# The setup of a fused RWKV and mixture-of-experts kernel in another order, and half of d v on GpSimd in units 1 to 3

## The chip, the cores and the metric

The kernel runs on one core of one Trainium2 chip. The metric is the device time of one execution in microseconds (us); smaller is better. The core has five engines that run beside each other, each through its own list of instructions in order: TensorE (PE; PEld is its weight load), VectorE (DVE), ScalarE (ACT), GpSimd (POOL) and SyncE (SP), which here issues the loads. An instruction waits on semaphores that other engines or finished loads raise, and everything behind it on its engine waits too.

## The reference

Two stages. The first is a linear-attention recurrence for 4 batches, 8 heads, 768 tokens and 48 columns a head. The second sends each of the 3072 token rows (384 wide) to one of 8 experts.

```python
for t in range(S):
    cur = u * k_t (outer) v_t
    y[t] = r_t @ (state + cur)
    state = w * state + k_t (outer) v_t
...
logits = x @ w_gate + modality_bias[modality_id]
e = argmax(logits)
out = prob[e] * (relu(x @ w1[e]) @ w2[e])
```

## The kernel before

The recurrence is computed in chunks of 128 tokens: 4 batches by 6 chunks are 24 units, taken in order 0 to 23 (all batches of chunk 0 first). For a unit, `rc` is r times decreasing powers of w (`powr`) and `kc` is k times increasing ones (`powk`), both with the head's columns on the partitions, two heads to a pair, four pairs (`NPR`) to a tile of 112 partitions by 4 x 128. `scores` multiplies `kc` by `rc` on TensorE into two PSUM banks, `causal` (VectorE) multiplies each by the mask into `at`, `values` (TensorE) multiplies `at` by v into `py`, then the keys `kt` by v into the state's bank `pst`, then `bonus`: the products of `rk` = k r with u, which give the eight numbers `d` of each token. `taken` copies `d` (ScalarE), `own` scales v by it head by head on ScalarE into `dv`, and `token` adds `dv` to `py` (VectorE) and squares it (ScalarE); `factor`, `high` and `low` make the scaled f16 halves of the row. In units of `SHARED` GpSimd makes the second half of `dv` in one product (`shared`) and ScalarE only the first.

From the first unit on, the engines' orders are written by hand (a manual schedule): what stands first in the program is first on its engine. One turn i of the loop over units issues, among others: `keys_turned(i+2)` (transposes of the key rows on TensorE), `scores(i+1)`, `taken(i)`, `shared(i)`, `token(i-1)`, `decay(i+3)` (`rc`, GpSimd), `carry(i+2)` (`kt`, GpSimd), `keys(i+2)` (VectorE), `own_turned(i+2)` (`rk`, VectorE, up to unit 3), `factor(i-1)`, `own(i)`, `high(i-1)`, `causal(i+1)`, `low(i-1)`, `values(i)`.

`setup` comes before the loop. In its program order it does, on each engine:

- SyncE: loads w, unit 0's turned rows (`turned(0)`, r and k, 384 KB into `ud0`), `turned(1)`, u in single elements (`uT`, 384 of them), then the k and v lines of units 0 to 2, `turned(2)`, the gate's weights, bias and modality; at its end unit 3's rows, `turned(4)`.
- VectorE: memsets (`ud0`'s unused rows among them), a running product of w (a scan), the reciprocal, the second half of `powk`, `w128`, then for unit 0 `kc` in two halves, the upper half of `rc`, `rk`, later `causal(0)`, `keys(1)`, `own_turned(1)`.
- ScalarE: its table load, the blank of `ud2`'s unused rows, three copies of powers into `powk` and `powr`, four `wk` scalings, blanks of `ud3`, of the four `kt` and of the state `st[1]`, the copy of `wtok`, `taken(0)`.
- GpSimd: the blank of `ud1`, identity and mask, `counts` (constants for the routing), the lower half of unit 0's `rc` in two quarters, `decay(1)`, the copies of u into `ub`, `carry(0)`, `decay(2)`, `uw`, `carry(1)`.
- TensorE: ten products on ones (`WARM`) that write nothing used, `scores(0)`, four transposes for `wtok`, `keys_turned(1)`, `bonus(0)`; in the loop's first turn `keys_turned(2)`, then three more products on ones (`DENSE`) ahead of `scores(1)`.

After the attention units the experts' weights are split and the rows of each expert are multiplied, mostly bound by TensorE; the change touches nothing there.

Of the kernel before, what the change touches and what calls it, by code (L numbers as in the profile page):

```python
# [37 lines left out]
NQ = 6  # L38
WARM = 10
NJ = 40  # L40
LATE = 5
SHARES = (0, 4), (4, 2), (6, 2)

DENSE = 6
FADED = range(4, 14)
SHARED = range(9, 14)
TURNED = (*range(1, 8), *range(12, 15))
RAISED = range(6, 12)
OWNED = range(17, 24)
GROUPED = 6  # L50
# [13 lines left out]
LOW, TOP = 64 - D, 64 + D  # L64
HALVES = slice(0, 64), slice(64, TOP)


class _Kernel:
# [16 lines left out]
    def setup(self):  # L85

        nc, c = self.nc, self.c
        w = c.tile([P, NPR], F32, name="w")
        nc.vector.memset(w, 1.0)
        nc.sync.dma_start(w[LOW:TOP, :], self.wT.rearrange("j d a -> (j d) a"))  # L90
        uT = c.tile([P, NPR], F32, name="uT")
        self.ud = [c.tile([P, 2 * NPR * P], F32, name=f"ud{q}") for q in range(4)]
# [3 lines left out]
        zero = c.tile([P, P // 2], F32, name="zero")  # L96
        nc.vector.memset(zero, 0.0)
        warm = self.warm = c.tile([P, 512], F16, name="warm")
        nc.gpsimd.memset(warm, 1.0)
        self.ones16 = warm[:, :P]  # L100
        for t in self.kv:
            nc.vector.memset(t[:, :LOW], 0.0)
        nc.vector.memset(self.ud[0][:LOW], 0.0)
        nc.gpsimd.memset(self.ud[1][:LOW], 0.0)
        H2 = P // 2
        blank = lambda t: nc.scalar.copy(t.rearrange("p (a z) -> p a z", z=P // 2), zero[: t.shape[0]].unsqueeze(1).to_broadcast([t.shape[0], t.shape[1] // (P // 2), P // 2]))
        self.tables = c.tile([P, 3, NPR, H2 + 1], F32, name="tables")
        wb, one0, pw = (self.tables[:, q] for q in range(3))
# [4 lines left out]
        nc.vector.memset(one0[:, :, 0:1], 1.0)  # L113
        nc.vector.memset(uT, 0.0)
        blank(self.ud[2][:LOW])
        self.turned(0)
        self.turned(1)
        nc.sync.dma_start(uT[LOW:TOP, :], self.u.rearrange("o (a z) -> z (o a)", a=NPR))
        self.lines(1, 0)
# [3 lines left out]
        for i in range(3):  # L123
            self.lines(i, 1)
        wg = c.tile([P, DC * E], F32, name="wgf")
        nc.sync.dma_start(wg, self.wg)
        bias = c.tile([P, 2 * E], F32, name="bias")
        nc.sync.dma_start(bias, self.bias.to_broadcast([P, 2 * E]))
        mod = c.tile([P, 2 * NT // P], I32, name="mod")
        nc.sync.dma_start(mod, self.mod)  # L130
        self.raw_in = wg, bias, mod

# [6 lines left out]
        self.ones = c.tile([P, P], F32, name="ones")  # L139
        nc.vector.memset(self.ones, 1.0)  # L140
        id32 = self.id32 = c.tile([P, P], F32, name="id32")
        make_identity(nc, id32)
        self.mask = c.tile([P, P], F32, name="mask")
        nc.gpsimd.affine_select(self.mask, self.ones, pattern=[[1, P]], compare_op=ALU.is_gt, fill=0.0, base=0, channel_multiplier=-1)
        self.counts()
        flat = lambda t: t.rearrange("p a z -> p (a z)")
# [14 lines left out]
        p64 = pw[:, :, H2 : H2 + 1].rearrange("p a o -> p (a o)")  # L161
        nc.vector.tensor_mul(self.w128, p64, p64)
        self.ub, self.uw = (c.tile([P, NPR, 2], F32, name=n) for n in ("ub", "uw"))
        self.decay(0, NPR, NPR // 2)
        self.keys(0, 2)
        u = self.ctx_[0]
        nc.vector.tensor_mul(u["rc"][:TOP, NPR // 2 :], u["rT"][:TOP, NPR // 2 :], self.powr[:TOP, NPR // 2 :])
        self.own_turned(0)
        self.decay(1)
        self.scores(0)  # L170
        self.wtok = c.tile([P, NPR, 2 * D], F32, name="wtok")
        wk = []
# [79 lines left out]
    def counts(self):  # L252

        c, v = self.c, self.nc.gpsimd
        self.onesb = c.tile([P, P], BF16, name="onesb")
        v.memset(self.onesb, 1.0)
        self.id16 = c.tile([P, P], F16, name="id16")
        make_identity(self.nc, self.id16)
        self.tok = c.tile([P, NT // P], I32, name="tok")
# [7 lines left out]
        self.base = c.tile([P, E], F32, name="base")  # L267
        v.tensor_copy(self.base, self.cbase)
        self.line = c.tile([P, 1], F32, name="line")
        v.tensor_copy(self.line, self.tok[:, 0:1])  # L270

# [56 lines left out]

    def turned(self, i):
# [5 lines left out]
        self.nc.sync.dma_start(ud[LOW:TOP, :m], self.pd[b * NCH + c].rearrange("j d n -> (j d) n")[:, :m])  # L335
        self.ctx_.setdefault(i, {}).update( rT=ud[:, :n].rearrange("p (a t) -> p a t", a=NPR), kT=ud[:, n:].rearrange("p (a t) -> p a t", a=NPR))
# [55 lines left out]

    def own_turned(self, i):
# [46 lines left out]
    def scores(self, i):  # L440
        nc, u = self.nc, self.ctx_[i]
        u["ps"] = [self.ps_a.tile([P, 512], F32, tag="big", name=f"psc{i}_{j}") for j in range(2)]
        if i == 1:

            for q in range(DENSE // 2):
                nc.tensor.matmul(u["ps"][q % 2], self.ones16, self.warm, start=True, stop=True)

        for pr in range(NPR):
            for q in range(2):
                s = slice(64 * q, 64 * q + 64)  # L450
                for j, r in enumerate(HALVES):
                    nc.tensor.matmul(u["ps"][j][s, pr * P : (pr + 1) * P], u["kc"][r, pr, s], u["rc"][r, pr, :], start=True, stop=True)  # L452
# [712 lines left out]
    def run(self):  # L1165
        nc, tc, m = self.nc, self.tc, self.m
# [233 lines left out]
        i, j = NU - 2, NU - 1  # L1400
# [208 lines left out]
```

## Time and profile before

| what | before |
|---|---|
| median of 3 runs | 334.5 us (333.94 to 335.64) |
| the profiled execution | 336.65 us |
| its span, first to last instruction | 334.6 us |
| busy: PE, PEld | 320.0 us (96%), 263.5 us (79%) |
| busy: DVE, ACT, POOL | 213.5 us (64%), 181.7 us (54%), 159.7 us (48%) |
| mean granted clock of TensorE | 0.994 |
| DMA | 48.71 MB, mean 146 GB/s |

The span is counted from the first instruction; the execution's time has about 2 us more around it. A busy share is an average over the whole span: the setup and the first units are some 30 us of it. Matmul ends are modelled, so a busy PE is not PE at its peak.

### The profile page before, as it was taken

The numbers are of one execution on the slowest core, as the hardware profiler recorded it, in microseconds if no ns is written. First come the engines' busy times: TensorE is split into PE (matmuls) and PEld (weight loads), VectorE is DVE, ScalarE is ACT, GpSimd is POOL, SyncE is SP. The second block draws the span as 40 slices with busy tenths as digits, with TensorE's granted clock in tenths as the row PEclk, the third lists the DMA queues.
The fourth block names the chain that finished last, engine by engine and source line by source line (L and its number), as shares of the span: only waits on it lengthen the run. The fifth ranks groups of instructions, "written<-read, shape, count | busy, mean of one in ns | idle before, by whom it ended". The sixth has DMA issues, their size and how long they took to land. (4 is left out here: it accounts for less than half of the span.)

```text
span 334.6 us, 15202 instructions
## 1 busy us (share of the span) xinstructions
PE 320.0 (96%) x5434; PEld 263.5 (79%) x5434; DVE 213.5 (64%) x727; ACT 181.7 (54%) x500; POOL 159.7 (48%) x241
## 2 busy tenths in 40 slices
PE   7999998998999999999999999999999999999992
PEld 2888897898978888797878788886888877777771
DVE  6878985899988988896667422286333332234950
ACT  7898888789655578676422222274222225543820
POOL 8978863967599886554458212203111111111211
PEclk9999999899999999999999999999999999999999
DMA  6879986995579999954246431119512211122110
GB/s 185 244 171 207 204 250 222 293 229 155 126 197 270 267 223 299 275 156 119 78 106 231 156 78 47 47 47 332 121 50 65 50 47 24 47 56 62 37 47 5
DMA packets 58013, 48.71 MB, mean 146 GB/s; under 512 B 42344, under 2 KB 50807, under 8 KB 57712
## 3 DMA queue, kind: packets, MB, share of 16 engines
q1 hardware_dynamic: 54768, 38.63, 47.5%
q0 software_dynamic: 3200, 9.47, 8.2%
q8 instruction: 30, 0.49, 0.7%
q14 instruction: 15, 0.12, 0.1%
HBM read 27.99 MB, written 11.83 MB: 119 GB/s over the span
## 5 line engine op out<-in xcount | busy, mean ns | idle before, releaser
L1067 PEld LDWEIGHTS <-whi 128*128 128x128 f16 x1248 | 72.6, 98 | 3.6 <-issue 0.7
L1076 DVE SCALAR_TENSOR_TENSOR hl<-phb,hh 128x256 f16<-128x256 f32 (+1 forms) x48 | 24.4, 508 | 66.8 <-ACTq L1540 66.8
L1130 PEld LDWEIGHTS <-hh 128*128 128x128 f16 x416 | 39.1, 98 | 25.3 <-ACT hh L1071 1.2
L1067 PE MATMUL phb<-mxT,whi 128*128 128x128 f16 x768 | 50.7, 219 | 0.0
L438 ACT ACTIVATE dv<-kv,d 128x48 f32<-128x48 f32 x172 | 43.0, 325 | 0.0
L1071 ACT ACTIVATE hh<-phb 128x256 f16<-128x256 f32 (+1 forms) x48 | 21.5, 455 | 32.4 <-PE phb L1067 22.9
L1067 PEld LDWEIGHTS <-wlo 128*128 128x128 f16 x624 | 37.8, 98 | 0.0
L1036 POOL TENSOR_TENSOR seenb<-otb,putb 128x1 int32<-128x1 int32 x16 | 4.1, 257 | 63.0 <-ACTq L1540 50.8
L458 DVE TENSOR_TENSOR at<-psc,mask 128x512 f32<-128x512 f32 x48 | 32.5, 681 | 1.5 <-PE psc L452 1.4
L1130 PEld LDWEIGHTS <-hl 128*128 128x128 f16 x208 | 19.8, 98 | 15.7 <-issue 2.5
L366 POOL TENSOR_TENSOR rc<-ud,powr 112x512 f32<-112x512 f32 (+1 forms) x25 | 30.8, 1237 | 0.2
L1027 ACT ACTIVATE otb<-po,fac 128x384 f32<-128x384 f32 x16 | 9.3, 580 | 39.5 <-PE phb L1067 39.5
L452 PE MATMUL psc<-rc,kc 64*64 64x128 f32 (+1 forms) x768 | 28.5, 281 | 1.2 <-POOL rc L366 1.0
L701 POOL DMA_INDIRECT rows<-row,posi x24 | 24.6, 1026 | 10.2 <-issue 3.6
L1067 PE MATMUL phb<-mxT,wlo 128*128 128x128 f16 x384 | 29.3, 219 | 0.0
L1130 PE MATMUL po<-whi,hl 128*128 128x384 f16 x136 | 28.0, 326 | 1.2 <-PEq L1605 0.7
L1130 PE MATMUL po<-whi,hh 128*128 128x384 f16 x136 | 27.7, 326 | 0.6 <-ACT hh L1071 0.4
L489 PE MATMUL py<-kv,at 128*64 128x48 f32 x768 | 27.0, 222 | 1.2 <-issue 1.2
L1067 PE MATMUL phs<-mxT,whi 128*128 128x128 f16 x432 | 27.3, 219 | 0.6 <-issue 0.6
L1130 PE MATMUL po<-wlo,hh 128*128 128x384 f16 x136 | 27.7, 326 | 0.0
L452 PEld LDWEIGHTS psc<-rc,kc 64*64 64x64 f32 (+1 forms) x768 | 21.9, 135 | 6.5 <-issue 2.5
L489 PEld LDWEIGHTS py<-kv,at 128*64 128x64 f32 x768 | 25.3, 138 | 2.1 <-issue 1.8
(292 smaller groups left out, 625.6 us busy)
## 6 DMA issues: line engine op xcount, KB each, us to landing
kv<-in_pt SPq DMA_DIRECT2D x21, 384.0 KB, 4.8
ud<-in_pd SPq DMA_DIRECT2D x14, 384.0 KB, 5.4
raw<-in_w SPq DMA_DIRECT2D x12, 256.0 KB, 5.1
raw<-in_w SPq DMA_DIRECT2D x6, 512.0 KB, 5.2
raw<-in_w SPq DMA_DIRECT2D x2, 1536.0 KB, 6.5
rows<-pad SPq DMA_DIRECT2D x10, 193.0 KB, 3.6
ud<-in_pd SPq DMA_DIRECT2D x10, 192.0 KB, 3.8
rt<-in_pt SPq DMA_DIRECT2D x7, 192.0 KB, 5.2
```

Source lines behind the costliest of these rows:

```text
L366: nc.gpsimd.tensor_mul(u["rc"][:TOP, s], u["rT"][:TOP, s], self.powr[:TOP, s])
L438: nc.scalar.activation(u["dv"][:, sl], u["v"][:, sl], AF.Copy, scale=u["d"][:, h : h + 1])
L452: nc.tensor.matmul(u["ps"][j][s, pr * P : (pr + 1) * P], u["kc"][r, pr, s], u["rc"][r, pr, :], start=True, stop=True)
L458: nc.vector.tensor_mul(u["at"][:, j * NPR : (j + 1) * NPR, :], u["ps"][j].rearrange("p (q t) -> p q t", q=NPR), self.mask.unsqueeze(1).to_ ...
L489: nc.tensor.matmul(py[t, sl], u["at"][:, j * NPR + pr, t], u["v"][:, sl], start=c == h == 0, stop=h == H - 1, skip_group_check=True)
L701: i = nc.gpsimd.indirect_dma_start(out=self.rows, out_offset=bass.IndirectOffsetOnAxis(ap=u["posi"][:, b : b + 1], axis=0), in_=u["row"][: ...
L1027: self.nc.scalar.activation(ot, po[:, :DM], AF.Copy, scale=gf[:, t : t + 1])
L1036: i1 = nc.gpsimd.tensor_tensor(seen, ot[:, 0:1].bitcast(I32), idx, ALU.add)
L1067: self.nc.tensor.matmul(ph[:, q * P : (q + 1) * P], w[:, c0 : c0 + P], self.xT[:, xq, t * P : (t + 1) * P], start=i == q == 0, stop=i == l ...
L1071: self.nc.scalar.activation(self.hh[:, f0 : f0 + fb, t * P : (t + 1) * P], p3, AF.Relu)
L1076: self.nc.vector.scalar_tensor_tensor(self.hl[:, f0 : f0 + fb, r], p3, 0.0, self.hh[:, f0 : f0 + fb, r], ALU.max, ALU.subtract)
L1130: self.nc.tensor.matmul(po[:, :DM], h[:, f, t * P : (t + 1) * P], w[:, c0 : c0 + DM], start=first, stop=last)
```

## The change

Order and placement change; every result stays. `turned(0)` is issued by ScalarE's queue as its first instruction. u is loaded as 4 rows of 96 (`ux`), transposed by TensorE into PSUM (`psd`) and copied to `ub` by ScalarE. `first` writes unit 0's rows and keys in other pieces: GpSimd one quarter of `rc`, VectorE half of `kc`, half of `rc`, `w128`, half of `kc`, a quarter of `rc`; `scores(0)` takes the pairs in the order 0, 1, 3, 2. Unit 0's `rk` moves from VectorE to GpSimd, behind `decay(1)`. Blanks: `ud0` to ScalarE (from VectorE), `ud2` to GpSimd (from ScalarE), `ud3` and `st[1]` behind `taken(0)`, `kt` ahead of the powers. `counts` is cut in three: `numbers` stays, `masks` comes behind `rk`, the rest at the end. `keys_turned(2)` moves from the loop into the setup, ahead of `bonus(0)`. The three `DENSE` products and one of `WARM` go. The gate's weights, bias and modality are loaded behind unit 3's. `SHARED` gains units 1 to 3.

```diff
-WARM = 10
+WARM = 9
-DENSE = 6
-SHARED = range(9, 14)
+SHARED = (*range(1, 4), *range(9, 14))
...
-        uT = c.tile([P, NPR], F32, name="uT")
...
+        self.turned(0, nc.scalar)
+        self.turned(1)
+        ux = c.tile([NPR, TOP], F32, name="ux")
+        self.ub, self.uw = (c.tile([P, NPR, 2], F32, name=n) for n in ("ub", "uw"))
+        nc.gpsimd.memset(ux, 0.0)
+        nc.gpsimd.memset(self.ub, 0.0)
+        nc.sync.dma_start(ux[:, LOW:], self.u.rearrange("o (a z) -> (o a) z", a=NPR))
-        nc.vector.memset(self.ud[0][:LOW], 0.0)
...
-        nc.vector.memset(uT, 0.0)
-        blank(self.ud[2][:LOW])
-        self.turned(0)
-        self.turned(1)
-        nc.sync.dma_start(uT[LOW:TOP, :], self.u.rearrange("o (a z) -> z (o a)", a=NPR))
+        blank(self.ud[0][:LOW])
+        for t in self.kt:
+            nc.scalar.copy(t[:, :, :LOW], zero[:, : NPR * LOW].rearrange("p (a z) -> p a z", a=NPR))
...
-        nc.vector.memset(self.ones, 1.0)
+        nc.gpsimd.memset(self.ones, 1.0)
...
-        self.counts()
+        nc.gpsimd.memset(self.ud[2][:LOW], 0.0)
+        self.numbers()
...
-        nc.vector.tensor_mul(self.w128, p64, p64)
-        self.ub, self.uw = (c.tile([P, NPR, 2], F32, name=n) for n in ("ub", "uw"))
-        self.decay(0, NPR, NPR // 2)
-        self.keys(0, 2)
-        u = self.ctx_[0]
-        nc.vector.tensor_mul(u["rc"][:TOP, NPR // 2 :], u["rT"][:TOP, NPR // 2 :], self.powr[:TOP, NPR // 2 :])
-        self.own_turned(0)
+        self.first(p64)
         self.decay(1)
+        self.own_turned(0, nc.gpsimd)
         self.scores(0)
...
-        blank(self.ud[3][:LOW])
-        for t in self.kt:
-            nc.scalar.copy(t[:, :, :LOW], zero[:, : NPR * LOW].rearrange("p (a z) -> p a z", a=NPR))
+        self.masks()
+        psd = self.ps_s.tile([P, 512], F32, tag="s", name="psd")
+        nc.tensor.transpose(psd[:TOP, :NPR], ux, id32[:NPR, :NPR])
+        for j, r in enumerate(HALVES):
+            nc.scalar.copy(self.ub[r, :, j], psd[r, :NPR])
+        self.keys_turned(1)
         pt = self.ps_y.tile([P, 512], F32, tag="y", name="pwk")
...
+        self.causal(0, 0)
+        self.keys(1)
+        self.causal(0, 1)
+        self.own_turned(1)
+        self.keys_turned(2)
+        self.bonus(0, psd)
+        self.taken(0)
+        blank(self.ud[3][:LOW])
         blank(self.st[1].rearrange("p b a e -> p (b a e)"))
-        nc.gpsimd.memset(self.ub, 0.0)
-        for j, r in enumerate(HALVES):
-            nc.gpsimd.tensor_copy(self.ub[r, :, j], uT[r])
-        self.keys_turned(1)
-        self.causal(0, 0)
-        self.causal(0, 1)
-        self.keys(1)
-        self.own_turned(1)
         self.carry(0)
         self.decay(2)
...
-        self.bonus(0, pst)
-        self.taken(0)
         self.carry(1)
+        self.counts()
         self.feed(3)
+        wg = c.tile([P, DC * E], F32, name="wgf")
+        nc.sync.dma_start(wg, self.wg)
         self.turned(4)
...
+    def first(self, p64):
+
+        nc, u, half = self.nc, self.ctx_[0], NPR // 2
...
+        part = lambda eng, out, x, pw, s: eng.tensor_mul(u[out][:TOP, s], u[x][:TOP, s], pw[:TOP, s])
+        lo, hi = slice(0, half), slice(half, NPR)
+        part(nc.gpsimd, "rc", "rT", self.powr, slice(NPR - 1, NPR))
+        part(nc.vector, "kc", "kT", self.powk, lo)
+        part(nc.vector, "rc", "rT", self.powr, lo)
+        nc.vector.tensor_mul(self.w128, p64, p64)
+        part(nc.vector, "kc", "kT", self.powk, hi)
+        part(nc.vector, "rc", "rT", self.powr, slice(half, NPR - 1))
...
-        self.nc.vector.tensor_mul(u["rk"][:TOP], u["kT"][:TOP], u["rT"][:TOP])
...
+        (by or self.nc.vector).tensor_mul(u["rk"][:TOP], u["kT"][:TOP], u["rT"][:TOP])
...
-        if i == 1:
-
-            for q in range(DENSE // 2):
-                nc.tensor.matmul(u["ps"][q % 2], self.ones16, self.warm, start=True, stop=True)
-
-        for pr in range(NPR):
+        for pr in range(NPR) if i else (0, 1, 3, 2):
...
-            if i < GROUPED:
+            if 0 < i < GROUPED:
                 each(i + 2, self.keys_turned)
```

## Rows read from the trace of the kernel before

**Rows 1.** Windows: stretch, its us, busy us of PE, PEld, DVE, ACT, POOL, clock, DMA.

```profile
30.00:40.00 10.00, 9.67 (x287) 9.00 (x282) 9.29 (x36) 7.81 (x32) 7.99 (x10) 1.00 1.01 205
```

**Rows 2.** Timeline of the setup, TensorE: start, us, engine, line, operation, idle before.

```profile
8.07 0.42 PEld L182 LDWEIGHTS pwk<-id,wk 128*128 128x128 f32 x4 [0.17 <-ACT kt L179]
9.09 0.55 PEld L413 LDWEIGHTS psd<-ub,rk 112*64 112x64 f32 x16 [0.18 <-POOL ub L187]
10.04 0.42 PEld L446 LDWEIGHTS <-warm 128*128 128x128 f16 x3
10.88 1.10 PE L452 MATMUL psc<-rc,kc 64*64 64x128 f32 x32
11.92 0.20 PEld L489 LDWEIGHTS py<-kv,at 128*64 128x64 f32 x4 [0.17 <-issue]
```

**Rows 3.** Timeline of the setup and turns 0 and 1, ScalarE.

```profile
0.80 1.28 ACT L106 ACT_TABLE_LOAD   x1 [0.67 <-PEq L1602]
4.86 0.41 ACT L159 COPY powr<-powk 128x256 f32<-128x256 f32 x1
6.35 1.03 ACT L106 COPY ud<-zero 16x1024 f32<-16x1024 f32 x1
7.28 0.68 ACT L179 COPY kt<-zero 128x64 f32<-128x64 f32 x4
9.14 1.48 ACT L106 COPY st<-zero 128x1536 f32<-128x1536 f32 x1
10.51 0.17 ACT L421 COPY d<-psd 128x8 f32<-128x8 f32 x1
10.72 1.91 ACT L438 ACTIVATE dv<-kv,d 128x48 f32<-128x48 f32 x8
14.00 0.64 ACT L544 COPY st<-pst 64x192 f32<-64x192 f32 x2 [1.16 <-PE pst L413]
14.71 0.50 ACT L529 ACTIVATE row<-py 128x384 f16<-128x384 f32 x1
```

**Rows 4.** Timeline of turns 1 to 4: the chain of VectorE and ScalarE.

```profile
17.34 0.68 DVE L458 TENSOR_TENSOR at<-psc,mask 128x512 f32<-128x512 f32 x1
18.53 0.49 ACT L529 ACTIVATE row<-py 128x384 f16<-128x384 f32 x1
21.83 0.62 DVE L566 SCALAR_TENSOR_TENSOR row<-py,sx,row 128x384 f16<-128x384 f32 x1 [1.73 <-ACT row L562]
26.55 0.85 PEld L452 LDWEIGHTS psc<-rc,kc 48*64 48x64 f32 x30 [0.47 <-DVE at L458]
```

**Rows 5.** DMA from 1.5 to 3.5 us in slices of 0.05, and SyncE's first rows.

```profile
GB/s 0 0 0 0 0 0 0 0 0 1 5 5 8 4 6 2 0 0 0 0 492 246 82 82 246 82 82 246 0 0 0 328 819 82 328 819 82 82 819 410
...
1.44 0.88 SPq L335 DMA_DIRECT2D ud<-in_pd  x2
```

**Rows 6.** Timeline of the setup: VectorE and GpSimd at unit 0's rows.

```profile
5.61 0.42 DVE L167 TENSOR_TENSOR rc<-ud,powr 112x256 f32<-112x256 f32 x1
5.70 0.64 POOL L366 TENSOR_TENSOR rc<-ud,powr 112x128 f32<-112x128 f32 x1
5.95 0.94 DVE L397 TENSOR_TENSOR rk<-ud 112x512 f32<-112x512 f32 x1
```

**Rows 7.** Instructions of line 404 (ns min/median/max), and a meeting at 98.6 us.

```profile
L404 DVE TENSOR_TENSOR kc<-ud,powk x15: 418/684/1546, 4.9 to 144.6; 112x512 f32<-112x512 f32 x13, 112x256 f32<-112x256 f32 x2
...
98.61 1.28 POOL L366 TENSOR_TENSOR rc<-ud,powr 112x512 f32<-112x512 f32 x1
98.95 1.50 DVE L404 TENSOR_TENSOR kc<-ud,powk 112x512 f32<-112x512 f32 x1
```

**Rows 8.** Timeline of TensorE at 54 to 59 us, and a window with the granted clock.

```profile
54.72 0.55 PE L489 MATMUL py<-kv,at 128*64 128x48 f32 x11 [1.17 <-issue]
56.91 2.17 PE L452 MATMUL psc<-rc,kc 64*64 64x128 f32 x32
...
58.00:59.00 1.00, 1.00 (x20) 0.68 (x14) 1.00 (x5) 1.00 (x2) 0.83 (x2) 0.50 0.98 249
```

More of the change, by code (lines that the diff above doesn't have):

```diff
@@ L124, in setup @@
             self.lines(i, 1)
[L125 to L131, printed above, removed]
         pt = self.ps_a.tile([P, 512], F32, tag="big", name="pwarm")
@@ L195, in setup @@
         nc.gpsimd.tensor_mul(self.uw, self.ub, w.unsqueeze(2).to_broadcast([P, NPR, 2]))
-        pst = self.ps_s.tile([P, 512], F32, tag="s", name="psd")
-        self.bonus(0, pst)
-        self.taken(0)
         self.carry(1)
+        self.counts()
         self.feed(3)
+        wg = c.tile([P, DC * E], F32, name="wgf")
+        nc.sync.dma_start(wg, self.wg)
         self.turned(4)
+        bias = c.tile([P, 2 * E], F32, name="bias")
+        nc.sync.dma_start(bias, self.bias.to_broadcast([P, 2 * E]))
+        mod = c.tile([P, 2 * NT // P], I32, name="mod")
+        nc.sync.dma_start(mod, self.mod)
+        self.raw_in = wg, bias, mod
+    def first(self, p64):
+        nc, u, half = self.nc, self.ctx_[0], NPR // 2
+        u["rc"] = self.a.tile([P, NPR, P], F32, tag="rc", name="rc0", bufs=4)
+        u["kc"] = self.a.tile([P, NPR, P], F32, tag="kc", name="kc0")
+        part = lambda eng, out, x, pw, s: eng.tensor_mul(u[out][:TOP, s], u[x][:TOP, s], pw[:TOP, s])
[6 more added lines that the diff above has]
+        part(nc.vector, "rc", "rT", self.powr, slice(half, NPR - 1))
     def setup2(self):
@@ L254, in counts, with masks @@
         c, v = self.c, self.nc.gpsimd
+        self.base = c.tile([P, E], F32, name="base")
+        v.tensor_copy(self.base, self.cbase)
+        self.line = c.tile([P, 1], F32, name="line")
+        v.tensor_copy(self.line, self.tok[:, 0:1])
+    def masks(self):
+        c, v = self.c, self.nc.gpsimd
         self.onesb = c.tile([P, P], BF16, name="onesb")
@@ L258, in counts, with numbers @@
         make_identity(self.nc, self.id16)
+    def numbers(self):
+        c, v = self.c, self.nc.gpsimd
         self.tok = c.tile([P, NT // P], I32, name="tok")
@@ L266, in counts @@
         self.idx, self.rev, self.cbase = (ci[:, q] for q in range(3))
[L267 to L270, printed above, removed]
     def setup5(self):
@@ L327, in feed, with turned @@
         self.lines(i)
-    def turned(self, i):
+    def turned(self, i, by=None):
         b, c = self.units[i]
@@ L334, in turned @@
         m = n if i in TURNED else 2 * n
-        self.nc.sync.dma_start(ud[LOW:TOP, :m], self.pd[b * NCH + c].rearrange("j d n -> (j d) n")[:, :m])
+        (by or self.nc.sync).dma_start(ud[LOW:TOP, :m], self.pd[b * NCH + c].rearrange("j d n -> (j d) n")[:, :m])
         self.ctx_.setdefault(i, {}).update( rT=ud[:, :n].rearrange("p (a t) -> p a t", a=NPR), kT=ud[:, n:].rearrange("p (a t) -> p a t", a=NPR))
@@ L359, in pace, with decay @@
         self.nc.values_load(ap[:1].bitcast(I32)[:, :1], engines=SP, skip_runtime_bounds_check_because="the value is not used, only the time at which it is there")
-    def decay(self, i, n=1, of=None):
+    def decay(self, i):
         nc, u = self.nc, self.ctx_[i]
         u["rc"] = self.a.tile([P, NPR, P], F32, tag="rc", name=f"rc{i}", bufs=4)
-        for q in range(of or n):
-            s = slice(q * NPR // n, (q + 1) * NPR // n)
-            nc.gpsimd.tensor_mul(u["rc"][:TOP, s], u["rT"][:TOP, s], self.powr[:TOP, s])
+        nc.gpsimd.tensor_mul(u["rc"][:TOP], u["rT"][:TOP], self.powr[:TOP])
     def carry(self, i):
@@ L391, in own_keys, with own_turned, keys @@
         nc.gpsimd.tensor_mul(u["rk"][:TOP], u["rc"][:TOP], u["kc"][:TOP])
-    def own_turned(self, i):
+    def own_turned(self, i, by=None):
         u = self.ctx_[i]
         u["rk"], u["uw"] = self.a.tile([P, NPR, P], F32, tag="rk", name=f"rk{i}"), self.ub
-        self.nc.vector.tensor_mul(u["rk"][:TOP], u["kT"][:TOP], u["rT"][:TOP])
-    def keys(self, i, n=1):
+        (by or self.nc.vector).tensor_mul(u["rk"][:TOP], u["kT"][:TOP], u["rT"][:TOP])
+    def keys(self, i):
         nc, a, u = self.nc, self.a, self.ctx_[i]
         u["kc"] = a.tile([P, NPR, P], F32, tag="kc", name=f"kc{i}")
-        for q in range(n):
-            s = slice(q * NPR // n, (q + 1) * NPR // n)
-            nc.vector.tensor_mul(u["kc"][:TOP, s], u["kT"][:TOP, s], self.powk[:TOP, s])
+        nc.vector.tensor_mul(u["kc"][:TOP], u["kT"][:TOP], self.powk[:TOP])
     def bonus(self, i, pst):
```

## The prediction, made before the change was timed

> **What bounds the kernel now.** I read the page's shares first, then the windows of 10 us, then each engine's timeline of the first 28 us. The reader is to see that TensorE is busy nearly all the time once the units run [rows 1], so whatever the setup gains or loses at TensorE is carried to the end: of ten microseconds it is busy in 9.67 there. The setup itself is read from three timelines. TensorE finishes loading for unit 0's scores at 8.07, does the `wtok` transposes, `pkT1`, the bonus products at 9.09, `pkT2`, three products that write nothing from 10.04 to 10.88, unit 1's scores from 10.88, and unit 0's values from 11.92 [rows 2].
>
> The second thing to see is that TensorE is not alone in setting the pace. From the square of unit 0 (`token`, ScalarE, 14.71) [rows 3] until unit 5's scores (26.55) two engines hand one chain to and fro: causal mask (VectorE, 17.34), add, square (ScalarE, 18.53), first half of `own`, `high`, `low` (VectorE, 21.83, after 1.73 us of waiting for ScalarE), causal mask again, and so on; at 26.55 TensorE has waited 0.47 us for that mask, whose PSUM buffer it needs [rows 4]. So the hour that counts is when unit 0's square starts (14.71), not when unit 0's values start.
>
> **The change, part by part.** The time is built on the profiled execution: a span of 334.6 us, 336.65 us with what lies around it. The median of the runs shown is 334.5 us; I add the change of the span to that median. About 0.5% (1.7 us) is what a measurement of this kernel can tell from no change.
>
> *The powers.* ScalarE now issues unit 0's load first: 0.44 us, half of what SyncE's two took [rows 5]. Then come the table load (from 0.80, 1.28 us), one blank (0.93 from its start to the next one's) and the four blanks of `kt` (0.68) [rows 3]: free at 0.80 + 0.44 + 1.28 + 0.93 + 0.68 = 4.13. The three copies of powers, 0.41 us each, end at 4.13 + 3 x 0.41 = 5.36, or near 5.2 if they overlap a little; before, the last ended at 5.27 [rows 3]. VectorE loses a memset of `ud0` and so may come to its power table earlier, if w is there: w's packets moved from 1.95 to 2.3, alone [rows 5]. No row shows two load queues at once, so the price of ScalarE's load beside w is bounded only. At best it is 0. At worst w lands with the last of unit 0's 384 KB: these start moving at 1.85 (1.06 after their issue, as SyncE's from 1.44 to 2.5) and take 1.4 us at 266 GB/s, the mean of the last 20 slices of that row, so w is there at 3.3 instead of 2.3 [rows 5]. Part of that microsecond is VectorE's spared memset; I hold 5.6 for the powers as the late end, and take 5.4. The Trainium skill (DMA: Bandwidth & Descriptors, section Queues, rings and completion order) says that each DMA engine goes round between its queues a packet at a time, which would put w's small packets behind large ones and the powers at the late end, 5.6; no run here shows it yet.
>
> *Rows and keys of unit 0 (`first`).* This is the part on which the sum turns. Before, VectorE's `rc` (5.61), GpSimd's first quarter (5.70) and VectorE's `rk` (5.95) met, and two of them stretched: the quarter took 0.64 us, and `rk` 0.94 against about 0.68 for such a product [rows 6, 7]. At 98.95 the reader sees it plainly: `kc`, a product of two SBUF tiles with a median of 0.684, took 1.50 us, that is, it began only when GpSimd's 1.28 us product of 98.61 was nearly over [rows 7]. They take turns, whoever asked first.
>
> In the new order VectorE still owes `w128`, the upper half of `kc` and a quarter of `rc` after its first `rc` half, all from SBUF, while GpSimd goes from its quarter into `decay(1)` and then `own_turned(0)`, 1.28 us each and SBUF only. With t0 = 5.4 (powers there): `rc` half to t0+0.36, GpSimd's quarter to +0.60, `w128` to +0.68; there `decay(1)` is waiting already and holds until +1.85, so `kc` runs to +2.2, `own_turned(0)` to +3.4, and the last quarter of `rc` to +3.65. Holds are the durations of [rows 6, 7] less some 0.1 us of tail, which is when the next was seen to begin. Eight products of unit 0's scores are left (about 0.3): TensorE goes on at t0+3.95 = 9.35 instead of 8.07.
>
> The order hangs on a tenth of a microsecond: `decay(1)` asks at +0.68, `kc` at +0.8 behind `w128`. If `w128` (four columns) took no turn, `kc` would come first, then `decay(1)`, and TensorE would go on at t0+2.7 = 8.1. If nobody waited, at t0+1.5 = 6.9. I take the first, because in [rows 6] the waiting engine was served next each time. The Trainium skill (SBUF — State Buffer, section SBUF: two separate sides) states this as a lock held for a whole instruction, for any VectorE operation with two SBUF inputs, `w128` too; by it the first order holds and 9.35 stands, without it for `w128` 8.1.
>
> *TensorE after that.* u's transpose (0.1), `pkT1` and `wtok` (1.02 less 0.18 of waiting, from 8.07 to 9.09), `pkT2` (0.45, as half of those two) [rows 2]: bonus at 9.35 + 0.1 + 0.84 + 0.45 = 10.75. It needs `rk` from GpSimd, there at t0+3.4 = 8.8. It takes 0.63, and ScalarE's copy `d0` follows at 11.4; before it was at 10.51. The three products that write nothing (0.84, 10.04 to 10.88) and one warm-up product are gone; worth nothing here, as TensorE then waits for masks, worth 0.84 where it sets the pace.
>
> *ScalarE after d0.* Before, the blanks of `ud3` and `st` lay in its idle time ahead of `d0`; now they are behind it. Before, ScalarE took 2.33 us for `d0`, `own(0)` and the square of wg (10.51 until it fell idle, 1.16 us ahead of 14.00) and 0.71 for the state copies and `d1` (14.00 to 14.71). Now `ud3` (0.93) and `st` (1.37, 9.14 to 10.51) come between: 2.33 + 0.93 + 1.37 + 0.71 = 5.34 us from `d0` to the square of unit 0 [rows 3]. The square starts at 11.4 + 5.34 = 16.75 instead of 14.71: 2.05 us late.
>
> *Half of d v on GpSimd.* Four `own` products leave ScalarE in units 1 to 3 (half of the eight that took 1.91 us, 0.96 a unit) [rows 3]; GpSimd gets 192 columns a unit, 0.48 by the 1.28 of 512 columns [rows 7]. In the chain, what follows `high` on ScalarE (0.96 + 0.71 = 1.67) runs beside VectorE's `low` (0.62) and the mask and add that lead to the square (17.34 to 18.53, 1.19), 1.81 together [rows 3, 4]; so its removal shortens nothing, and where ScalarE was last all the same, at most its 0.96. On GpSimd the half waits for `d`, and the next `decay`, `carry` and `own_keys` queue behind it; rows are made two units ahead, so I cost that at 0. If that cover were gone, each half would cost its 0.48.
>
> *Loads, `numbers`, `masks`, `counts`.* u in 4 rows instead of 384 elements, wg, bias and mod behind unit 3's and 4's loads: needed after 12.5 us, so 0. `ud4` now waits for GpSimd's `rk` (8.8) and the loads queued behind it on SyncE with it; unit 4's keys are wanted after 17 us, so 0.
>
> **Sum.** 334.5 + 2.05 = 336.55, say 336.5 us. Its own range is 336.2 to 336.9 (t0 from 5.2 to 5.6).
>
> **Rivals.**
> *B, one turn lost.* `kc` gets in before `decay(1)`: TensorE goes on at 8.1, `d0` at 10.15, the square at 15.5, 0.8 late: 335.3. For it: the tenth of a microsecond above. Against: [rows 6].
> *C, nobody waits.* TensorE goes on at 6.9; the bonus then waits for GpSimd's `rk` (8.3), `d0` is at 9.0, the square at 14.35: 0.35 early, 334.15, not slower. It decides if `decay(1)` comes over 1.2 us after t0, as when unit 1's rows land late. Against it: those loads start early.
> *D, TensorE's gain passes whole.* As in C, unit 0's values start at 10.1 instead of 11.92. If ScalarE, relieved of 0.96 a unit, is what held the chain, that 1.8 us is carried: 332.7. The point from which it decides: the square of unit 0 by 12.9. For it: ScalarE is full in those units; against it: the 5.34 us behind `d0`.
> *E, the clock falls.* In the first order TensorE has two holes of over 1 us between 6 and 9.4. After the 1.17 us hole that ended at 54.72 the granted clock was 0.50 at 58 to 59, the 1.2 GHz level, and a unit's scores took 2.17 us instead of 1.10 [rows 2, 8]. The scores alone lost 1.07 us there; with a second, shorter group in such a stretch I put its cost at 1.7 (an estimate from that row). Unit 0's values would be 1 us late where the square is 2.05 late, so 1 us of it is hidden and about 0.7 is added: 337.2.
>
> **Chances.** The first order 0.34, E 0.08, B 0.18, C 0.18, D 0.22. Slower by over 0.5%: 0.34 + 0.08 = 0.42; within 0.5%: B and C, 0.36; faster: D, 0.22. The range runs from D's 332.7 to 337.3, just past E; it leaves out D's lower half and what E may add. The likeliest case alone is 336.2 to 336.9.
>
> **What would show it.** `kc`'s upper half and the last `rc` quarter on VectorE over 1 us long, beside `decay(1)` and `own_turned(0)`; unit 0's last scores after 9 us; `d0` near 11.4 and the square near 16.7; the 0.47 us wait of unit 5's scores still there, some 2 us later. Wrong if those two products take 0.42 and 0.25 us; if the powers end before 5.1 or after 5.7; if ScalarE has idle time between `d0` and the square; or if the 1.17 us hole before 54.72, which has no releaser, moves with the new instruction count and takes its clock fall along.

## The result, and the profile after

The change made the kernel slower: 338.75 us, median of 6 runs (337.55 to 345.77), against 334.72 of 6 runs before (333.94 to 335.64); ratio 1.0127, 95% interval 1.0084 to 1.0169. Forecast were 336.5 us and a range of 332.7 to 337.3. The sign was right, the loss was twice as large. Ratios are over undisturbed runs: one that is over 1.5% above the fastest of its kernel is left out.

The timeline of the changed kernel answers to [rows 2 to 4] (start, us, engine, line, operation, idle before and what ended it):

```profile
0.82 0.40 ACTq L356 DMA_DIRECT2D ud<-in_pd  x1
0.98 0.41 SPq L89 DMA_DIRECT2D w<-in_wT  x1
...
4.54 0.29 DVE L143 COPY tables<-w 128x256 f32<-128x256 f32 x1 [2.67 <-DMA w<-in_wT]
6.45 0.41 ACT L155 COPY powr<-powk 128x256 f32<-128x256 f32 x1
7.36 1.16 PEld L464 LDWEIGHTS psc<-rc,kc 64*64 64x64 f32 x24 [2.86 <-DVE rc L207]
7.59 1.52 POOL L385 TENSOR_TENSOR rc<-ud,powr 112x512 f32<-112x512 f32 x1
7.90 1.35 DVE L207 TENSOR_TENSOR rc<-ud,powr 112x128 f32<-112x128 f32 x1
9.31 0.30 PEld L464 LDWEIGHTS psc<-rc,kc 64*64 64x64 f32 x8 [0.79 <-DVE rc L207]
10.13 1.10 PE L375 MATMUL pkT<-id,kv 128*112 128x128 f32 x4
13.59 0.17 ACT L438 COPY d<-psd 128x8 f32<-128x8 f32 x1 [0.99 <-PE psd L430]
13.66 1.04 ACT L110 COPY ud<-zero 16x1024 f32<-16x1024 f32 x1
14.60 1.47 ACT L110 COPY st<-zero 128x1536 f32<-128x1536 f32 x1
15.98 1.90 ACT L455 ACTIVATE dv<-kv,d 128x48 f32<-128x48 f32 x8
17.92 0.57 DVE L522 TENSOR_TENSOR py<-py,dv 128x384 f32<-128x384 f32 x1 [2.00 <-ACT dv L455]
18.69 0.50 ACT L541 ACTIVATE row<-py 128x384 f16<-128x384 f32 x1
30.53 0.86 PEld L464 LDWEIGHTS psc<-rc,kc 48*64 48x64 f32 x30 [0.58 <-DVE at L470]
```

Three rows of the kernel before that answer to them:

```profile
2.98 0.23 DVE L147 COPY tables<-w 128x256 f32<-128x256 f32 x1
7.25 0.64 PEld L452 LDWEIGHTS psc<-rc,kc 64*64 64x64 f32 x24 [0.65 <-POOL rc L366]
8.07 0.66 PE L182 MATMUL pwk<-id,wk 128*128 128x128 f32 x4
```

Read the first list downwards. VectorE waits 2.67 us for w, so the last copy of powers ends at 6.86 and not at 5.27. TensorE's weight load waits 2.86 us for unit 0's `rc`, and 0.79 us more for the last quarter of `rc`, which took 1.35 us on VectorE beside GpSimd's 1.52. Four transposes then take 1.10 us, and `d0` is at 13.59 where it was at 10.51 [rows 3]. The square of unit 0 (18.69) is 3.98 us later than before, unit 5's scores too (26.55 to 30.53) [rows 4], and the median is 4.03 us longer. The profiled span grew by only 1.9 us (334.6 to 336.5). The two traces tell where the rest went: at unit 10's scores the changed kernel is 3.83 us behind, at unit 12's 1.33. Between them lie the hole and the fall of the clock of [rows 8], which the execution that was profiled before had and this one has not; at unit 23's scores it is 1.58 behind.

TensorE's clock has a part in it. By the trace's clock record it was first granted in full at 6.03 us before, and at 12.99 us after, 7.58 us behind the end of the warm-up products (5.41). Ahead of its first record the windows print 1.00 with nothing behind it, so durations show it: four such transposes took 0.66 us before (8.07), as in the runs below whose clock was up by then, and 1.10 here.

### The profile page after: what moved, and what is told of

Same layout as the page of the kernel before. It is cut to its first block, busy times and chain, and to the rows that moved or that the text cites. A ratio compares the mean times of both kernels' runs of the same rounds, so it can differ in the third digit from the quotient of the medians.

```text
span 336.5 us, 15195 instructions
## 1 busy us (share of the span) xinstructions
PE 319.4 (95%) x5431; PEld 263.3 (78%) x5431; DVE 213.7 (63%) x724; ACT 179.5 (53%) x490; POOL 163.4 (49%) x245
## 5 line engine op out<-in xcount | busy, mean ns | idle before, releaser
L455 ACT ACTIVATE dv<-kv,d 128x48 f32<-128x48 f32 x160 | 39.9, 324 | 0.0
L713 POOL DMA_INDIRECT rows<-row,posi x24 | 25.4, 1057 | 10.3 <-issue 3.4
L385 POOL TENSOR_TENSOR rc<-ud,powr 112x512 f32<-112x512 f32 x23 | 29.7, 1290 | 0.2
```

The lines of the kernel that those rows point to most:

```text
L385: nc.gpsimd.tensor_mul(u["rc"][:TOP], u["rT"][:TOP], self.powr[:TOP])
L455: nc.scalar.activation(u["dv"][:, sl], u["v"][:, sl], AF.Copy, scale=u["d"][:, h : h + 1])
L713: i = nc.gpsimd.indirect_dma_start(out=self.rows, out_offset=bass.IndirectOffsetOnAxis(ap=u["posi"][:, b : b + 1], axis=0), in_=u["row"][: ...
```

## The experiments

Each kernel was compared with the kernel before in the same group of runs, as times of unchanged kernels moved by up to 5 us from one group to the next. This table is read from the timeline of each run's profiled execution (us), one trace a row. "Copy" is VectorE's first copy from w; "wait" that of TensorE's weight load inside unit 0's scores; "clock full" when the trace's record first has the clock in full ("4.74 to 8.16, 18.40": it fell at 8.16 and came back at 18.40); "unit 5" the load of unit 5's scores behind the wait for the mask. In h2 no load waits there: 26.81 is the first of the 32, the one that answers to the others' is at 27.23.

| run | copy | wait | clock full | d0 | unit 5 | d0 to unit 5 | ratio |
|---|---|---|---|---|---|---|---|
| before | 2.98 | 0.65 | 6.03 | 10.51 | 26.55 | 16.04 | 1 |
| after | 4.54 | 0.79 | 12.99 | 13.59 | 30.53 | 16.94 | 1.0127 |
| f1 | 4.60 | 0.79 | 17.60 | 13.99 | 31.35 | 17.36 | 1.0076 |
| e1 | 2.65 | 0.81, 0.88 | 17.36 | 13.80 | 31.15 | 17.35 | 1.0004 |
| e1b | 2.70 | 1.12, 0.93 | 4.74 to 8.16, 18.40 | 13.85 | 31.62 | 17.77 | |
| e1c | 2.74 | 0.30, 0.98 | 5.32 to 8.74, 15.56 | 12.05 | 29.35 | 17.30 | |
| e2 | 4.53 | 0.31, 0.98 | 5.32 | 11.97 | 28.96 | 16.99 | 1.0066 |
| e3 | 4.55 | 0.79 | 13.58 | 13.86 | 29.55 | 15.69 | 1.0114 |
| e4 | 4.61 | 0.78 | 13.79 | 13.99 | 30.97 | 16.98 | 1.0125 |
| e5 | 2.99 | 0.39 | 4.08 | 10.00 | 26.68 | 16.68 | 1.0001 |
| f5 | 2.98 | 0.39 | 4.36 | 10.03 | 26.50 | 16.47 | 0.9967 |
| f2 | 2.65 | 0.70 | 6.29 | 10.49 | 27.42 | 16.93 | 0.9981 |
| f3 | 2.78 | none | 5.52 | 9.91 | 26.83 | 16.92 | 1.0002 |
| g1 | 2.66 | 0.31, 0.98 | 4.22 to 7.63, 11.04 | 11.96 | 28.78 | 16.82 | 1.0177 |
| h1 | 4.63 | none | 16.78 | 13.36 | 30.61 | 17.25 | 1.0099 |
| h2 | 2.65 | 0.31 | 5.53 | 10.29 | 26.81 | 16.52 | 1.0004 |
| f4 | 2.65 | none | 4.26 | 10.26 | 25.93 | 15.67 | 0.9972 |
| g2 | 2.66 | none | 6.82 | 10.30 | 25.96 | 15.66 | 0.9986 |

**f1: the changed kernel once more.**

> The changed kernel itself once more, unaltered, so that the others of this group stand beside it on one chip. Both theories: 1.011 to 1.014 of the time before. For the theory that TensorE's clock is one of the two terms: VectorE's copy from w at 4.5 us again, and the clock's rise after 8 us in the clock's row in most executions; if the rise comes by 6 us here, unit 5's scores start near 29 us and not near 30.5.

Ratio 1.0076 (1.004 to 1.0112), below what was expected, though unit 5's scores are later than in the first trace, by 0.82 us, and `d0` by 0.40; VectorE's copy from w is late again, and the clock full at 17.60. So differences of under half a microsecond at `d0`, or of under 0.8 at unit 5, are not told by one trace of each kernel, nor ratios of 1.008 and 1.013 from each other.

**e1: unit 0's rows back on SyncE behind w.**

```diff
-        self.turned(0, nc.scalar)
+        self.turned(0)
```

> The changed kernel with unit 0's rows loaded by SyncE again, second behind w; all else as changed. Theory 1 (w's small packets wait behind unit 0's rows on the other queue): w moves at about 2.1 us instead of 3.2, VectorE's first product of powers comes at 3.0 instead of 4.54, the powers 1.5 us earlier, unit 0's square at 15.5 to 17 instead of 18.69 (the spread is whether TensorE's clock has risen by 8 us), unit 5's scores as much earlier than 30.53; the time falls by 1.5 to 3 us, to 335.7 to 337.2. Rival (w is late for another reason, such as the start of the execution): w lands at 4.5 as before, no change, 338.7.

Ratio 1.0004 (0.9965 to 1.0043). w is there 1.9 us earlier, yet `d0` is no earlier (13.80). The timeline of VectorE, GpSimd and TensorE shows why:

```profile
6.05 1.45 POOL L385 TENSOR_TENSOR rc<-ud,powr 112x512 f32<-112x512 f32 x1
6.29 1.22 DVE L212 TENSOR_TENSOR w<-tables 128x4 f32<-128x4 f32 x1
7.44 0.41 DVE L207 TENSOR_TENSOR kc<-ud,powk 112x256 f32<-112x256 f32 x1
7.77 1.35 DVE L207 TENSOR_TENSOR rc<-ud,powr 112x128 f32<-112x128 f32 x1
9.17 0.30 PEld L464 LDWEIGHTS psc<-rc,kc 64*64 64x64 f32 x8 [0.88 <-DVE rc L207]
```

Two turns are lost, as many as in the likeliest case of the forecast, but the first of them is that of `w128` and not of `kc`: its four columns took 1.22 us behind GpSimd's product (0.42 in the changed kernel behind a shorter one, 0.15 in f3 behind none). The ratio and this trace don't agree; two more profiled executions of the same kernel:

> A second look at the changed kernel with unit 0's rows back on SyncE, for its clock and its order of products alone. Theory 'with w early the pause before unit 0's scores is short and the clock comes up early in most executions': rise by 7 us and unit 5's scores at 27.3 to 28.8. If the rise comes after 8 us here too, an early w does not bring the clock up with 9 warm-up products, and the 1.2% that this version won in time must come from elsewhere.

> A third look at the same kernel, with the same expectation: rise by 7 us and unit 5's scores at 27.3 to 28.8, or else a late rise as in the first look (17.36) and unit 5's scores near 31.

They took 349.56 and 338.6 us, beside a median of 335.76 before. In both the clock came up early and fell again behind the wait, as the windows of the second of them (e1c) show (us, then busy time of PE, PEld, DVE, ACT, POOL, the granted clock, DMA):

```profile
6.00:8.00 2.00, 1.18 (x28) 0.72 (x29) 1.89 (x3) 1.28 (x4) 2.00 (x3) 1.00 1.07 336
8.00:10.00 2.00, 2.00 (x17) 1.81 (x18) 1.30 (x3) 0.31 (x2) 1.59 (x4) 0.68 1.06 341
10.00:12.00 2.00, 2.00 (x25) 1.64 (x25) 1.87 (x4) 0.48 (x1) 1.20 (x2) 0.50 1.07 277
```

Busy 1.18 of 2 us, then the 1.2 GHz level (0.50). None of the three profiled executions is as short as the median of the kernel before, and the median of all ten runs of e1 is 340.81 against 338.95. So its 1.0004 is not taken as a full recovery.

**e2: 14 warm-up products instead of 9.**

```diff
-WARM = 9
+WARM = 14
```

> The changed kernel with 14 products that write nothing at the start instead of 9, so that TensorE is busy up to its first scores (7.36 us). Theory 1 (1.4 us are lost because TensorE idles from 5.4 to 7.36 and again to 9.3 and so runs at 1.2 GHz until 13 us): the transposes of unit 1 and of the weights take 0.6 instead of 1.1 us, the copy of d0 comes 1.2 to 1.6 us earlier than 13.59, the square of unit 0 too; 337.1 to 337.5. Rival (the transposes are slow for their loads or data, not for the clock): they still take 1.1 us, no change, 338.7.

Ratio 1.0066 (1.0035 to 1.0098). w is as late as ever, the same turn is lost, but the clock is up and the transposes are short:

```profile
9.31 0.45 PE L464 MATMUL psc<-rc,kc 64*64 64x128 f32 x8 [0.74 <-DVE rc L207]
9.84 0.65 PE L375 MATMUL pkT<-id,kv 128*112 128x128 f32 x4
11.97 0.17 ACT L438 COPY d<-psd 128x8 f32<-128x8 f32 x1 [0.53 <-PE psd L430]
```

`d0` is 1.62 us earlier than in the changed kernel (2.02 than in f1): that is the clock's share in the traces. The times don't show it, as 1.0066 lies beside f1's 1.0076.

**e3: the blanks of ud3 and st ahead of the copies of u into ub.**

```diff
+        blank(self.ud[3][:LOW])
+        blank(self.st[1].rearrange("p b a e -> p (b a e)"))
         self.masks()
...
         self.taken(0)
-        blank(self.ud[3][:LOW])
-        blank(self.st[1].rearrange("p b a e -> p (b a e)"))
```

> The changed kernel with ScalarE's blanks of ud3 and of the state ahead of the copies of u, in its idle time from 9.0 us, instead of behind d0. Theory 1 (the blanks lie on the chain from d0 to unit 0's square): the copy of d0 stays within 0.3 of 13.59, the square comes 1.3 to 1.8 us earlier than 18.69 (then TensorE's bonus of unit 1, 16.5, and the state copies bound it), unit 5's scores as much earlier than 30.53; 337.0 to 337.4. Rival (the chain has slack behind the square, or TensorE alone sets the pace): square earlier, unit 5's scores within 0.3 of 30.53, 338.7.

Ratio 1.0114 (1.0084 to 1.0144), hardly less than the change itself; but in its trace `d0` to unit 5's scores takes 15.69 us and not 16.94, as `dv` follows `d0` at once (the time doesn't show these 1.25 us):

```profile
13.86 0.17 ACT L438 COPY d<-psd 128x8 f32<-128x8 f32 x1 [1.25 <-PE psd L430]
14.06 1.93 ACT L455 ACTIVATE dv<-kv,d 128x48 f32<-128x48 f32 x8
```

**e4 and e5: GpSimd's half of d v, taken away, and alone.**

```diff
-SHARED = (*range(1, 4), *range(9, 14))
+SHARED = range(9, 14)
```

> The changed kernel with units 1 to 3 not shared: ScalarE does all of d v there again. Theory 1 (the half of d v is on no path): unit 5's scores within 0.4 us of 30.53, the time within 0.5 of the changed kernel, 338.2 to 339.2. Rival (GpSimd's halves wait for d and make its later rows and keys late, which is where the loss behind 30 us comes from): GpSimd's rows of units 4 to 7 earlier by 1 us or more, and 1 us or more of time back, 337.5 or less.

Without it 1.0125 (1.0087 to 1.0164), 16.98 us from `d0` to unit 5. The other way round, in the kernel before:

> The kernel before, in which GpSimd does half of d v in units 1 to 3 and nothing else is changed. Prediction: nothing, ratio 0.997 to 1.003, and 16.0 us from d0 to unit 5's scores as before. Rival 'ScalarE held the chain': these 16.0 us shrink by up to 0.96, ratio 0.993 to 0.997. Rival 'GpSimd's rows come late': TensorE waits for rc or kt in units 3 to 8, ratio 1.003 to 1.01.

1.0001 (0.9969 to 1.0034), unit 5's scores at 26.68. It costs and brings nothing that the times can tell.

**f2 and f3: w early and 12 warm-up products; then GpSimd's constants first.** Over e1, f2 sets `WARM = 12`. f3 adds:

```diff
         self.first(p64)
+        self.masks()
         self.decay(1)
...
-        self.masks()
```

> The changed kernel with unit 0's rows back on SyncE behind w, and 12 warm-up products where it has 9. Theory 'w and the clock are two terms that add': ratio 0.998 to 1.004, the powers' last copy from 4.55 us, the clock up by 6 us, d0 at 11.2 to 11.9, unit 5's scores at 28 to 29. Rival 'the lock eats what w gives': the powers come 1.9 us earlier, but GpSimd's product for unit 1 then gets in ahead of VectorE's w128, two turns are lost and TensorE goes on near 9.1 as before: ratio 1.005 to 1.008, the same as with late w and a long warm-up.

> As the run with unit 0's rows on SyncE and 12 warm-up products, and GpSimd makes its two bf16 and f16 constants (0.7 us) before its product for unit 1 and not after its own keys of unit 0. If the lock between VectorE's and GpSimd's products is what holds TensorE near 9.1: VectorE's last quarter of rc takes 0.3 and not 1.35 us, TensorE's last eight scores of unit 0 start by 7.2, and unit 5's scores come 1 to 2 us earlier than there; ratio 0.993 to 1.0. If TensorE is held by something else (ScalarE's wk, the clock): under 0.3 us, ratio as there.

f2: 0.9981 (0.9924 to 1.0037). f3: 1.0002 (0.9962 to 1.0042). With early w and full clock the loss is gone; of the two f3 shows it more safely, as the median of all ten runs is 341.46 in f2 and 339.15 in f3, against 339.65 before. In f3 none of VectorE's products waits for GpSimd's product for unit 1, and TensorE takes all 32 scores at one go:

```profile
6.16 1.17 PE L464 MATMUL psc<-rc,kc 64*64 64x128 f32 x32
6.44 0.37 DVE L207 TENSOR_TENSOR rc<-ud,powr 112x128 f32<-112x128 f32 x1
6.64 1.31 POOL L385 TENSOR_TENSOR rc<-ud,powr 112x512 f32<-112x512 f32 x1
```

The quarter takes 0.37 us instead of 1.35, and `d0` is 0.58 us earlier; the time doesn't show that.

**f5: the kernel before with 9 warm-up products.** `WARM = 9` is its only edit.

> The kernel before with one warm-up product less (9 where it has 10), nothing else. Theory 'the one product that the change took away is what lost the clock's early rise': rise after 8 us in the profile, unit 5's scores 1 to 1.5 us later than 26.55, ratio 1.003 to 1.006. Rival 'the long pause before unit 0's scores, which the late w makes, is what lost it': rise at 6 us as before, ratio 0.998 to 1.002.

Ratio 0.9967 (0.993 to 1.0005), the clock full at 4.36, unit 5's scores at 26.50: in the order before, the product less costs nothing.

**h1 and h2: the lost turn alone taken away; then the late w too.** h1 is the changed kernel with f3's edit; h2 has e1's besides. Both have 9 warm-up products.

> The changed kernel with GpSimd's constants ahead of its product for unit 1 and nothing else: w still late, 9 warm-up products, but no product of VectorE's waits for one of GpSimd's. Theory 'TensorE's wait inside unit 0's scores costs 1.2 to 1.6 us itself and the clock another 1 to 1.6': TensorE takes unit 0's scores in one go from 7.4, d0 at 11 to 12.3, unit 5's scores at 27.9 to 29.2, the clock up by 11 us, ratio 1.003 to 1.008. If the pause that the late w makes ahead of the scores (5.41 to 7.4) is enough to keep the clock down: the scores in one go, but rise after 11 us all the same, d0 at 12.3 to 13, ratio 1.007 to 1.012.

> The same with unit 0's rows on SyncE, still 9 warm-up products: neither w nor a turn is lost, and only the blanks behind d0 and one warm-up product stand between it and the kernel before. Theory 'the wait inside unit 0's scores, not the number of warm-up products, is what takes the clock': rise by 7 us and no fall before 20, d0 at 9.9 to 10.3, unit 5's scores at 26.8 to 27.3, ratio 0.997 to 1.003, with few of its executions far above the rest. If 9 products are too few in this order: the clock low over most of 7 to 13 us, d0 near 12, unit 5's scores at 29 or later, ratio 1.004 to 1.012.

h1: 1.0099 (1.0049 to 1.0148), clock full at 16.78. h2: 1.0004 (0.9969 to 1.0039), clock full at 5.53 and not down before 26, median of all ten 336.05 against 336.09. First h1, then h2:

```profile
7.45 1.98 PE L464 MATMUL psc<-rc,kc 64*64 64x128 f32 x32 [2.04 <-DVE rc L207]
9.55 1.10 PE L375 MATMUL pkT<-id,kv 128*112 128x128 f32 x4
13.36 0.17 ACT L438 COPY d<-psd 128x8 f32<-128x8 f32 x1 [1.34 <-PE psd L430]
```

```profile
5.81 1.43 PE L464 MATMUL psc<-rc,kc 64*64 64x128 f32 x32 [0.39 <-DVE rc L207]
7.31 0.65 PE L375 MATMUL pkT<-id,kv 128*112 128x128 f32 x4
10.29 0.17 ACT L438 COPY d<-psd 128x8 f32<-128x8 f32 x1 [1.37 <-PE psd L430]
```

In time this pair is the clearest: h2 keeps all of the change but the late w and the order of GpSimd's constants, and the loss is gone; h1, in which w is still late, keeps most of it. At `d0` the two lie 3.07 us apart: 1.64 by the start of unit 0's scores (7.45 and 5.81), the rest behind it, where h1's clock is low.

What decides whether the clock comes up is not shown. With late w and nine warm-up products it came up at 12.99 us or later in all five traces (after, f1, e3, e4, h1); with early w and nine by 5.53 in five of six (e1b, e1c, f5, g1, h2). That looks as if the pause ahead of the scores (2.04 us in h1, 0.39 in h2) kept it down. But in these five it rose before unit 0's scores began (h2: 5.53 and 5.81), when TensorE had been given nothing but the nine products that h1 had from the same time on: a pause that came after can't have made that difference. The sixth, e1, is the same program as e1b and e1c and had its clock at 17.36. With ten or more products it was up by 6.82 in all seven traces. The fall is nearer to a wait: in e1b, e1c and g1 it came down at 8.16, 8.74 and 7.63, near a wait of 1.0 to 1.1 us inside the scores (ended at 8.01, 7.94 and 7.90); in e2, with 14 products, a wait of 0.98 was borne.

**g1: unit 0's rows by ScalarE, but issued behind w.**

```diff
+        nc.vector.memset(self.ud[0][32:64, :1], 0.0)
         self.turned(0, nc.scalar)
```

> The changed kernel with one tiny memset (one element of 32 partitions of unit 0's tile, rewritten by the load) ahead of unit 0's load, so that ScalarE issues it some 0.2 us after SyncE has begun to issue w and no longer 0.17 us ahead. Theory 'what was issued first moves first': w's packets move near 2.0 to 2.4 us, VectorE's copy from w starts by 2.8, the powers' last copy by 4.7, though unit 0's rows still come by ScalarE's queue; ratio 0.998 to 1.005. Rival 'small packets lose to large ones of another queue, whoever was first' (the two queues share): copy from w after 3.5 us, ratio 1.006 to 1.013.

The DMA queues from 2 to 3 us (packets, MB, share), first of the changed kernel, then of g1; `q10` is ScalarE's, `q1` SyncE's:

```profile
q10 hardware_dynamic: 70, 0.29, 88.3%
```

```profile
q10 hardware_dynamic: 37, 0.15, 61.1%
q1 hardware_dynamic: 111, 0.00, 5.2%
```

The two issues of g1, from its timeline:

```profile
0.98 0.41 SPq L89 DMA_DIRECT2D w<-in_wT  x1
1.18 0.40 ACTq L357 DMA_DIRECT2D ud<-in_pd  x1
```

In the changed kernel nothing of SyncE's queue moves in that microsecond: all 96 packets of w (16 bytes each) move from 3.11 to 3.54, as the last 12 of unit 0's 96 large packets start (up to 3.34). Behind the data each load has 16 small packets of 4 bytes; those of unit 0's rows start from 3.10 to 3.50, those of w from 3.14 to 3.54, each some 0.04 us behind one of the rows'. In g1 ScalarE issues at 1.18, 0.20 us behind SyncE's 0.98, and w's packets move from 2.00 to 2.30, ahead of the rows' (2.24 to 3.94). The copy from w starts at 2.66. So it is not the second queue as such that makes w late; what was issued first moved first. The ratio, 1.0177 (1.0108 to 1.0245) from 3 runs, is the miss of the set: unit 5's scores are at 28.78, earlier than in e2, and the rest of the loss comes later. Part of it, 1.13 us, is a wait for GpSimd's `rk` at 71.69; the changed kernel's trace has one of 1.36 us at 72.16, f1's none. What decides it was not found.

**f4 and g2: all terms undone.** f4 is f3 with the blank of `ud3` ahead of `wk` and that of `st` behind it; in g2 the gate's weights are loaded ahead of unit 3's rows as well.

```diff
         wk = []
+        blank(self.ud[3][:LOW])
...
             wk.append(t)
+        blank(self.st[1].rearrange("p b a e -> p (b a e)"))
...
-        self.feed(3)
         wg = c.tile([P, DC * E], F32, name="wgf")
         nc.sync.dma_start(wg, self.wg)
+        self.feed(3)
```

> As the run with GpSimd's constants first (unit 0's rows on SyncE, 12 warm-up products), and ScalarE's blanks of ud3 and st stand on both sides of its wk instead of behind d0. All three terms of the loss are then gone: d0 at 9.9 to 10.3, 15.7 us from d0 to unit 5's scores where the run it is built on has 16.9, so unit 5's scores at 25.6 to 26; ratio 0.992 to 0.998. If the terms do not add (ub or wtok come late behind the blanks, or the gain is given back by unit 10): unit 5's scores at 26.5 or later, ratio 0.998 to 1.002.

> As the run with the blanks early, and wg's load stands ahead of unit 3's loads on SyncE's queue and no longer behind them. There ScalarE's square of wg waited 0.81 us for it and the state copies and the square of unit 0 behind it. If that wait sets the chain: the square of unit 0 starts near 13.6 and not at 14.1, unit 5's scores at 25.5 to 25.7, and the ratio is 0.994 to 0.998. If TensorE is already the bound there (it waits only 0.15 us for the mask at unit 5): unit 5's scores at 25.8 or later, ratio as there, 0.996 to 0.999.

f4: 0.9972 (0.9944 to 1.0000), unit 5's scores at 25.93, 0.62 us ahead of the kernel before. g2: 0.9986 (0.9945 to 1.0027), 25.96. In g2 ScalarE's wait for the gate's weights (0.81 us) is gone, but the state copies then wait for TensorE:

```profile
12.32 0.21 ACT L225 ACTIVATE wgsq<-wgf 128x24 f32<-128x24 f32 x1
13.29 0.64 ACT L556 COPY st<-pst 64x192 f32<-64x192 f32 x2 [0.68 <-PE pst L430]
```

So TensorE is the bound there. f4 is the best version, but the interval of its 0.3% reaches 1, so a gain is not shown.

## Why the prediction was wrong

The loss at unit 5's scores, 3.98 us, splits by pairs of runs. Late w: e2 less f2, both at full clock and with one lost turn, 11.97 - 10.49 = 1.48. The clock: the change less e2, 13.59 - 11.97 = 1.62. The work behind `d0`: 16.94 - 16.04 = 0.90. What is left of the new order, f2 against before, is 10.49 - 10.51 = -0.02. Sum 3.98, by construction; each term is a difference of single traces and good to about 0.4. Undone singly the faults bring little: w early (e1) leaves `d0` at 13.80, 13.85 and 12.05, the turn alone (h1) at 13.36, both together (h2) bring it to 10.29.

- *The powers: the step that failed.* "I hold 5.6 for the powers as the late end, and take 5.4"; they were there at 6.86. w was put between 0 and 1 us late, there at 3.3 at worst; its last packet went at 3.54 and not 2.30, and VectorE started 1.0 us behind that packet instead of 0.35 (g1), as the last update of w's semaphore in the trace is at 4.51 (2.63 in g1). Why that took longer is open. I took w's small packets to go in turns with large ones. The order of issue, 0.16 us, decided for the whole load.
- *What hid it.* The forecast has the square of unit 0 at 16.75; it was at 18.69. In its own terms: powers 1.46 us later, one lost turn instead of two 1.25 less (9.35 - 8.1), the rest of the way to `d0` 1.98 more (most of it the clock), `d0` to the square 0.24 less. That the first two nearly cancel is luck; what carried the time past the range is the clock, which the sum had at nothing.
- The Trainium skill (DMA: Bandwidth & Descriptors, section Queues, rings and completion order) lets a DMA engine drain one whole packet of about 9 to 17 descriptors before it switches. The trace agrees if the rows that the profile calls packets, 7 an engine for unit 0's load, are descriptors of one such packet; I had read them as packets. Read so, the rule puts w behind the whole load, as measured (3.11 to 3.54).
- *Rows and keys of unit 0.* Turns are taken as described: 1.35 us for a quarter that takes 0.28 to 0.37 where it waits for none of GpSimd's products (h1, h2, f3). Which order came was left at a tenth of a microsecond, rightly: in the changed kernel one turn was lost (rival B's order: TensorE goes on 1.95 us behind its first scores), in e1 two. `w128` does take a turn (1.22 us).
- That even so small a product with two SBUF inputs is locked out agrees with the Trainium skill (SBUF — State Buffer, section SBUF: two separate sides).
- *The clock (rival E), the second step that failed.* Its price came near, 1.7 against 1.62 measured, but for another event: E has the clock fall behind two holes within the scores, while in the changed kernel it had not come up at all before 12.99. Its chance was put at 0.08, and all but 0.7 of it was held to be hidden, while here all of it lies ahead of `d0`.
- *ScalarE behind d0.* 5.10 us from `d0` to the square of unit 0 for the 5.34 forecast, without idle time; in the traces of e3 and f4 moving the blanks gives back 1.25 of them.
- *Warm-up products at nothing.* By the times right for the number alone (f5, h2); with late w five more of them were worth 1.62 us at `d0` in the trace (e2).
- *d v on GpSimd and the carrying to the end.* The first as forecast: nothing (e4, e5). The second holds roughly: 3.98 us at unit 5 for 4.03 in the median, but 4.80 for 3.16 in f1's group, so that the close agreement of the first pair is chance.

Rivals C and D did not occur. Open are e1's ratio beside its three traces, g1's, and what decides when the clock comes up.

## What to carry to other kernels

A load that moves to another queue can hold up a tiny one that everything waits for: look at the order of issue over all queues, not within one. In a chain that starts from such a load, keep the clock in the sum: where it was not up when TensorE began, that cost as much again here (1.62 us beside 1.48). Where two faults stand in one chain, undo them together as well as singly: e1 and h1 alone brought little in their traces, h2 all. And when one engine must not meet another on SBUF, give it other work for that stretch (0.7 us of constants) rather than counting on who comes first; in the traces that was worth 0.58 us at `d0`.

## What was not expected of the hardware

Two loads issued 0.16 us apart on two queues were served one after the other, 384 KB ahead of 1.5 KB: w's first packet moved when 84 of the 96 large ones had begun. And the hour from which the clock stays full moved by 4.6 us between executions of one program (12.99 and 17.60 for the changed kernel; 17.36, 18.40 and 15.56 for e1). Two of e1's three had it in full from about 5 to 8 us as well, the third did not. So one trace doesn't tell a kernel's usual clock in its first 20 us.
